# Two token tiles of the gated MLP move, for two thirds of d_ff, from plain products to steps of seven block products

## The chip, the cores and the metric

One core of a Trainium2 chip. The metric is the time of one execution on the device in microseconds; the kernel before is given as the median of three runs. The engines are TensorE (PE in the profile, its weight loads PEld), VectorE (DVE), ScalarE (ACT), GpSimd (POOL) and SyncE (SP), which issues the DMAs of this kernel.

## The reference

Attention with a memory, then a gated MLP on its output. B=4, H=8, S=576, D=64, so 2304 tokens of 512; d_ff is 1536. q, k, v, M_prev and z_prev are float32, w_a, w_b and w_out are float64, and the result is float32.

```python
def _attn_ref(q, k, v, M_prev, z_prev, beta):
    scores = scale * np.matmul(q, k.transpose(0, 1, 3, 2))
    scores = np.where(causal, -1000000000.0, scores)
    scores = scores - scores.max(-1, keepdims=True)
    a = np.exp(scores)
    a /= a.sum(-1, keepdims=True) + 1e-09
    local = np.matmul(a, v)
    q_p = phi(q)                       # phi(x) = where(x > 0, x, exp(x) - 1) + 1
    mem_ret = np.einsum('bhsd,bhde->bhse', q_p, M_prev)
    mem_norm = np.einsum('bhsd,bhd->bhs', q_p, z_prev)[..., None] + 1e-06
    g = 1.0 / (1.0 + np.exp(-beta))[None, :, None, None]
    return g * (mem_ret / mem_norm) + (1 - g) * local

def _moe_ref(x, w_a, w_b, w_out):
    return (((x @ w_a) * (x @ w_b)) @ w_out).astype(np.float32)
```

## The kernel before

**Arithmetic.** A float32 operand is split into a high part, which TensorE reads as it is, and the rest, and a product is three matmuls: high by high, high by low, low by high. ScalarE copies out the high part, VectorE subtracts it (`split_lo`, line 224).

**Order.** No scheduler runs. Every operation has a short name, and a text lists `name.index` in the order of issue, the same list for all engines; each engine takes its own in that order and waits on the others by semaphores. `HEAD`, `LOOP` and `TAIL` are that text (`schedule` unrolls `LOOP`), and after it `step7` is called in a Python loop.

**Attention (0 to 205.5 us).** Sixteen pairs of heads in a software pipeline of some 70 names a pair. The local part of each pair goes to `xs` in DRAM (`st_`). Towards its end the first unit of weights is converted.

**Weights.** The 24 units n (two for each of the twelve blocks f of 128 columns of d_ff: a with b, 128x1024, and out, 128x512) come as raw float64 by `load` and pass `mag` (ScalarE, line 883, from the raw words into the buffer `wt`, of which there is one for each kind), `clamp` (GpSimd), `shift`, `high`, `low` (VectorE, 903 and its neighbours), `hi` (ScalarE, 922) and `lo` (VectorE, 224). hi and lo write the split weights `wh`, `wl`, which stay on the chip. The next `mag` into a `wt` waits for the `lo` of the one before.

**Columns.** Tokens are cut in tiles of 384: tiles t = 0 to 3 are tokens 0 to 1535. A column (t, f) is `uA` and `uB` (`half`, line 945: twelve matmuls 128x384 each, h transposed, d_ff on partitions), `ucx` (ScalarE, a copy of b's sum to SBUF), `umx` (VectorE, times a's), `uhh`, `uhl` (the split of h) and `uo` (`outer`, line 983: nine matmuls 128x512 into three PSUM banks that hold the tile's output rows over all f; `written` carries them out). There are 48: tiles 0 and 1 by twelve f, then tiles 2 and 3 by twelve f. Until about 310 us the columns of tiles 0 and 1 run beside the conversion of the weights.

**Memory units.** Tiles 2 to 5 (tokens 768 to 2303) get their memory part from 16 units (t, j): `memory_unit`, names `q_load` to `q_join_l`. A unit loads q, z and the two halves of x, makes phi (VectorE's part at line 1131), the norm (a sum, four copies of 32x12 at line 1154, an addition, a reciprocal), transposes, splits, retrieves on TensorE, and joins (1200) the result to the sum of the two halves of x that GpSimd made (`sums`). In tiles 2 and 3 the rows are then split for the columns (`q_join_h`, `q_join_l`).

**Seven-product steps.** Tokens 1536 to 2303 (768) are multiplied by a and b in twelve calls of `step7(f)`, in Strassen and Winograd's form: the halves of x over d_model and tokens (B11 to B22) and four sums of them (T1, TT2, T4, T3; `combine`, `split_x`) against the blocks a11 to a22 (w_a and w_b, halves of d_model) and four sums s1 to s4. A product `part` is six matmuls of 384, seven in place of eight. For the sums, VectorE adds the split weights together again (`Wf`, 24 times 128x512), SP stores them (`Ws`, to `ws`), they are loaded (`sums_load`), GpSimd adds blocks (`sums_of`) and ScalarE and VectorE split them. Three sums of products begin from `p1`, the first product, which ScalarE copies to SBUF (line 1354) for VectorE to add (1371 and others). Four blocks of 128 rows of the output leave in the step (`out_rows`, 1425); the other two of each f are kept split (`kept`) and multiplied at the end (`late_rows`, 1456).

```python
        al = bank("ab")
        part(al, a11, B11, True)
        p1 = pools["w2"].tile([P, TB], F32, tag="x", name="x", bufs=1)[:, 0:TH]
        nc.scalar.activation(out=p1, in_=al, func=AF.Copy)
        ...
        be = bank("ab2")
        part(be, s2, TT2, True)
        u2 = tmp("u2")
        nc.vector.tensor_tensor(out=u2, in0=be, in1=p1, op=ALU.add)
        ...
        ga = bank("ab")
        part(ga, s1, T1, True)
        part(al, a12, B21)
        part(be, s3, T3)
```

Of the kernel before, what the change touches and what calls it, by code (L numbers as in the profile page):

```python
# [30 lines left out]
BANKS = """
0123450125341450231452304203541203541032014312345021340250432452310542305103253152401352014025124153
0421504305145341203541032014312340521430250123502301543120534513045305142013540241052405412351042532
1543254213041523403142034231052425310312401324501324015354123120543532041354014235034120512
"""
LOOP = """
Lt:-1 mag2:3 me:3 H1:2 shift1:3 b_3:1 S_3:1 py:4 m3A:1 v_l:2 low2:3 mc:1 hh:4 e4:2 h3A:3 TQ:0 thQ:0
pe:3 TK:0 H0:3 l3A:3 lo0:2 V1A:3 r_:2 V2A:3 b_:1 mx:3 tlQ:0 b_2:1 e3A:1 lo1:4 m3B:1 S_2:1 n0:2
mag1:2 ma:0 thK:0 S_:1 xA:3 V1B:3 shift2:3 n1:2 tlK:0 m2B:1 st_:4 e3B:1 Tq:0 pc:2 m2A:1 V2B:3 pb:2
n2:2 e2B:1 Lp:1 hl:4 n4:2 e2A:1 high2:3 n3:2 Lk:-2 high0:2 clamp0:2 mb:0 mB:1 eB:1 px:4 v_h:1 G2A:2  # L40
sq:-1 thq:0 G1:2 mA:1 LM:2 hi1:4 G0:2 pd:2 xB:3 h2A:2 h0:2 G2B:2 md:1 tlq:0 G5:2 high1:3 shift0:2
mu:0 h5:2 S_4:1 l2A:2 h2B:2 clamp2:3 l5:2 l2B:2 h1:2 G4:2 clamp1:3 l1:2 m4:1 eA:1 cx:3 w_0:2 pf:3
G3B:2 sm:3 hi0:2 h3B:2 h4:2 low1:3 low0:2 pa:1 Lv:0 l0:2 l3B:2 mag0:1 l4:2 G3A:2
/
clamp2 md hh v_l H1 e4 pe me mag2 Lt low2 h3A px sq mb b_3 S_3 pb Lk TQ V1A pf m3A l3A TK thQ shift2
V2A clamp1 b_ pc tlQ r_ pd b_2 e3A thK mc Lv S_2 S_ mag1 py n1 clamp0 m3B m2A V1B Lp n4 n2 Tq xA n3
m2B e3B n0 e2A H0 tlK st_ shift0 e2B thq V2B high1 mB G5 v_h mA mag0 G1 tlq eB G2B G2A xB lo1 h5 h2B
l5 h2A G4 sm S_4 l2B shift1 h1 hi0 l2A h4 G0 h0 eA w_0 l1 low1 l4 LM G3A G3B high2 pa hi1 h3B m4
high0 mx mu low0 cx hl lo0 ma l3B l0
"""  # L50
SPAN = (3, 9, 14)
TAIL = """
h3A.11 TK.14 b_3.13 l3A.11 S_3.13 pd.12 e4.12 r_.12 px.10 n3.12 pe.11 thK.14 pb.12 m3B.13 pf.11
pc.12 TQ.14 V1A.11 V2A.11 tlK.14 n1.12 m3A.13 e3B.13 thQ.14 fw.0 b_.13 b_2.13 S_2.13 n4.12 xA.11
m2A.13 Lp.13 m2B.13 e3A.13 e2A.13 S_.13 V1B.11 n0.12 e2B.13 mA.13 py.10 G5.12 V2B.11 eA.13 mB.13
tlQ.14 n2.12 G0.12 h5.12 G1.12 xB.11 l5.12 G3A.12 h1.12 v_l.12 G4.12 h3A.12 h4.12 h0.12 G2A.12
S_4.13 eB.13 pe.12 px.11 pa.13 h2A.12 v_h.13 G2B.12 w_0.12 pb.13 b_3.14 l1.12 l3A.12 h2B.12 l4.12
m4.13 py.11 S_3.14 G3B.12 l2A.12 pf.12 e4.13 TQ.15 m3A.14 r_.13 l0.12 pc.13 V1A.12 h3B.12 l2B.12
V2A.12 st_.10 thQ.15 pd.13 e3A.14 b_.14 px.12 Lv.15 l3B.12 n3.13 b_2.14 S_.14 xA.12 S_2.14 TK.15
m3B.14 n4.13 tlQ.15 Tq.14 V1B.12 n1.13 e3B.14 mA.14 V2B.12 eA.14 m2A.14 thq.14 m2B.14 e2A.14 tlq.14  # L60
G5.13 n0.13 G4.13 thK.15 mB.14 G3A.13 tlK.15 pe.13 G0.13 S_4.14 eB.14 h5.13 l5.13 n2.13 xB.12 h4.13
G1.13 h0.13 v_l.13 pf.13 Lp.14 b_3.15 pd.14 S_3.15 e2B.14 l4.13 w_0.13 m4.14 h3A.13 Tq.15 G2A.13
h1.13 l0.13 l3A.13 e4.14 thq.15 G3B.13 st_.11 l1.13 Lv.14 r_.14 h2A.13 G2B.13 m3B.15 h2B.13 V1A.13
l2A.13 e3B.15 py.12 v_h.14 n3.14 V2A.13 b_2.15 v_l.14 n4.14 b_.15 l2B.13 tlq.15 n1.14 S_2.15 m3A.15
px.13 h3B.13 l3B.13 S_.15 xA.13 e3A.15 m2B.15 pa.14 m2A.15 e2B.15 V1B.13 V2B.13 n0.14 mB.15 v_h.15
mA.15 e2A.15 pb.14 G3B.14 v_l.15 G4.14 G3A.14 eB.15 n2.14 xB.13 h3B.14 G0.14 pc.14 h4.14 l3B.14
S_4.15 G1.14 G5.14 h0.14 w_0.14 m4.15 h3A.14 eA.15 G2A.14 e4.15 h1.14 l0.14 l4.14 G2B.14 l3A.14
r_.15 to.0 pe.14 l1.14 pf.14 h5.14 h2A.14 n3.15 V1A.14 mag0.15 h2B.14 l2A.14 l5.14 n0.15 clamp0.15
n4.15 V2A.14 l2B.14 V1B.14 n2.15 n1.15 mag1.15 shift0.15 high0.15 V2B.14 xA.14 low0.15 G5.15 G2A.15
st_.12 h2A.15 G2B.15 px.14 clamp1.15 G3A.15 h5.15 G0.15 G4.15 hi0.15 h0.15 G1.15 G3B.15 l2A.15  # L70
w_0.15 h4.15 h3A.15 l5.15 lo0.15 st_.13 h1.15 l4.15 shift1.15 l1.15 H1.15 h3B.15 l3A.15 l0.15 l3B.15
xB.14 mag2.15 cx.15 V1A.15 clamp2.15 shift2.15 h2B.15 py.14 high1.15 V2A.15 l2B.15 H0.15 V1B.15
py.13 high2.15 V2B.15 low1.15 mx.15 st_.14 xA.15 xB.15 hh.15 hl.15 st_.15 low2.15 pp.0 hi1.15 lo1.15
uA.1 Khi.2 Kload.7 Kmag.3 Kload.6 uB.1 Klo.2 Kclamp.3 ucx.1 Kshift.3 Khigh.3 uA.2 Kload.8 Kmag.4
# [86 lines left out]
def kernel(  # L161
# [1465 lines left out]
```

## Time and profile before

| | us |
|---|---|
| median of three runs | 656.33 (655.96 to 656.79) |
| the profiled execution | 658.8 |
| its span in the trace | 656.9 |
| attention, up to | 205.5 |
| columns beside the conversion of the weights | 205.5 to 310 |
| columns alone, the last with the first step | 310 to about 522 |
| one seven-product step in the steady state | 10.07 |

All rows are of the profiled execution. The page's first part gives the busy time of each engine, its fourth the chain of work that ended last, its sixth the DMA issues. The windows give the same busy times for a stretch, with the granted clock of TensorE, the DMA engines' share and the GB/s moved. A group by line has the busy time and the mean of one in ns, then the idle time before and what ended it.

### The profile page before, as it was taken

The numbers are of one execution on the slowest core, as the hardware profiler recorded it, in microseconds if no ns is written. First come the engines' busy times: TensorE is split into PE (matmuls) and PEld (weight loads), VectorE is DVE, ScalarE is ACT, GpSimd is POOL, SyncE is SP. The second block draws the span as 40 slices with busy tenths as digits, with TensorE's granted clock in tenths as the row PEclk, the third lists the DMA queues.
The fourth block names the chain that finished last, engine by engine and source line by source line (L and its number), as shares of the span: only waits on it lengthen the run. The fifth ranks groups of instructions, "written<-read, shape, count | busy, mean of one in ns | idle before, by whom it ended". The sixth has DMA issues, their size and how long they took to land.

```text
span 656.9 us, 11557 instructions
## 1 busy us (share of the span) xinstructions
PE 644.9 (98%) x4010; PEld 592.4 (90%) x4010; DVE 510.8 (78%) x1018; ACT 338.0 (51%) x806; POOL 278.2 (42%) x402
## 2 busy tenths in 40 slices
PE   9999999999989999999999999999999999999998
PEld 6788889899878899999999999998999899999987
DVE  6999998988889888898997667477776676768740
ACT  6999999999976454454133223234223423123310
POOL 4999999999994122112402020011011443113200
PEclk9999999999999999999999999999999999999999
DMA  8956646466641454552445243234311321111001
GB/s 184 201 132 181 172 116 180 139 172 212 188 176 73 164 190 135 185 193 49 113 146 148 78 143 96 75 74 118 69 41 33 103 74 65 64 33 65 0 33 65
DMA packets 130250, 76.85 MB, mean 117 GB/s; under 512 B 98704, under 2 KB 117392, under 8 KB 130192
## 3 DMA queue, kind: packets, MB, share of 16 engines
q1 hardware_dynamic: 130192, 76.12, 41.0%
q8 instruction: 32, 0.52, 0.3%
q14 instruction: 26, 0.21, 0.1%
HBM read 55.64 MB, written 20.45 MB: 116 GB/s over the span
## 4 chain that ended last, share of the span: by engine, by line
PE 66%; DVE 15%; POOL 8%; ACT 6%; issue 3%; DMA 1%; SPq 1%; ACTq 0%; POOLq 0%; DVEq 0%
PE pp L945 22%; PE pp L1340 12%; PE o L983 10%; PE pt L220 5%; PE pw L734 4%; PE o L1425 4%; POOL P L634 4%; PE pt L568 3%; DVE PT L224 3%; PE pr L1456 3%; DVE wl L224 2%; DVE nm L607 2%; DVE wt L903 1%; PE m L1425 1%; POOL xf L1299 1%
## 5 line engine op out<-in xcount | busy, mean ns | idle before, releaser
L945 PE MATMUL pp<-xh,wh 128*128 128x384 f32 x376 | 127.2, 338 | 1.9 <-ACT x L958 1.1
L945 PE MATMUL pp<-xh,wl 128*128 128x384 f32 x376 | 126.1, 335 | 0.0
L945 PE MATMUL pp<-xl,wh 128*128 128x384 f32 x376 | 125.9, 335 | 0.0
L634 POOL TENSOR_SCALAR P<-P,sum 128x256 f32<-128x256 f32 (+4 forms) x144 | 82.1, 596 | 2.7 <-ACT ph L299 1.6
L1299 POOL TENSOR_TENSOR xf<-xf 128x256 f32<-128x256 f32 x48 | 39.8, 830 | 90.7 <-DMA xf<-ws 58.0
L945 PEld LDWEIGHTS pp<-xh,wh 128*128 128x128 f32 x376 | 70.6, 188 | 6.6 <-ACT x L958 3.2
L945 PEld LDWEIGHTS pp<-xl,wh 128*128 128x128 f32 x376 | 70.6, 188 | 1.3
L945 PEld LDWEIGHTS pp<-xh,wl 128*128 128x128 f32 x376 | 70.6, 188 | 0.0
L617 ACT ACTIVATE P<-pt,nm 128x128 f32<-128x128 f32 (+3 forms) x128 | 67.1, 534 | 6.7 <-DVE nm L607 3.5
L224 DVE TENSOR_TENSOR PT<-pt,PT 128x512 fp32r<-128x512 f32 (+2 forms) x112 | 62.7, 588 | 9.3 <-ACT PT L689 8.2
L734 PE MATMUL pw<-PT,vh 128*128 128x448 f32 (+4 forms) x352 | 64.1, 319 | 1.5 <-ACT xo L743 0.8
L734 PEld LDWEIGHTS pw<-PT,vh 128*128 128x128 f32 x352 | 55.9, 189 | 6.9 <-DVE PT L224 2.0
L607 DVE TENSOR_REDUCE nm<-pt 128x1 f32<-128x384 f32 (+3 forms) x128 | 55.7, 478 | 3.6 <-PE pt L568 3.1
L983 PE MATMUL o<-wh,hl 128*128 128x512 f32 x144 | 56.9, 395 | 0.0
L983 PE MATMUL o<-wl,hh 128*128 128x512 f32 x144 | 56.7, 394 | 0.0
L983 PE MATMUL o<-wh,hh 128*128 128x512 f32 x144 | 56.1, 390 | 0.0
L220 PE MATMUL pt<-ident,P 128*128 128x128 f32 (+1 forms) x400 | 52.7, 275 | 2.8 <-POOL P L634 1.4
L689 ACT ACTIVATE PT<-pt 128x512 fp32r<-128x512 f32 (+2 forms) x112 | 53.0, 529 | 3.0 <-PE pt L220 3.0
L889 POOL TENSOR_SCALAR wt<-wt 128x512 f32<-128x512 f32 (+1 forms) x21 | 21.3, 1012 | 75.5 <-ACT wt L883 75.5
L958 ACT ACTIVATE x<-pp 128x384 f32<-128x384 f32 x47 | 22.9, 487 | 56.8 <-DVE hl L224 33.9
L965 ACT ACTIVATE hh<-x 128x384 fp32r<-128x384 f32 x48 | 25.1, 522 | 49.3 <-DVE x L961 28.2
L220 PEld LDWEIGHTS pt<-ident,P 128*128 128x128 f32 (+1 forms) x400 | 43.8, 140 | 6.3 <-POOL P L634 4.3
(214 smaller groups left out, 1556.2 us busy)
## 6 DMA issues: line engine op xcount, KB each, us to landing
xs<-xo SPq DMA_DIRECT2D x16, 576.0 KB, 4.2
xx<-xs SPq DMA_DIRECT2D x32, 192.0 KB, 3.5
wr<-in_moe_w_a_dram SPq DMA_DIRECT2D x12, 512.0 KB, 4.8
wr<-in_moe_w_b_dram SPq DMA_DIRECT2D x12, 512.0 KB, 5.8
wr<-in_moe_w_out_dram SPq DMA_DIRECT2D x12, 512.0 KB, 3.9
ws<-fw SPq DMA_DIRECT2D x24, 256.0 KB, 2.3
xf<-ws SPq DMA_DIRECT2D x12, 512.0 KB, 3.2
qr<-in_q_dram SPq DMA_DIRECT2D x34, 128.0 KB, 3.4
```

Of the source, the lines that this page charges most:

```text
L220: nc.tensor.transpose(out, x, ident[0:x.shape[0], 0:x.shape[0]])
L224: eng.tensor_tensor(out=lo, in0=x, in1=hi, op=ALU.subtract)
L607: nc.vector.tensor_reduce(out=s["nm"][:, c:c + 1], in_=src, axis=AX.X, op=ALU.min)
L617: nc.scalar.activation(out=s["P", i][:, h, :], in_=src, func=AF.Exp, scale=-1.0, bias=s["nm"][:, c:c + 1], accum_out=s["sums"][:, c, 0:1],)
L634: nc.gpsimd.tensor_scalar(out=pr[:, h, :], in0=pr[:, h, :], scalar1=r[:, c:c + 1], scalar2=1.0, op0=ALU.mult, op1=ALU.mult,)
L689: nc.scalar.activation(out=dst, in_=src, func=AF.Copy)
L734: nc.tensor.matmul(pv[:, a:hi], lhsT=w, rhs=x, start=(n == 0), stop=(n == len(ops) - 1))
L945: nc.tensor.matmul(pp, lhsT=w[:, w0:w0 + P], rhs=x[:, kk, :], start=(c == 0), stop=(c == 3 * KK - 1),)
L983: nc.tensor.matmul(po[t, m], lhsT=hx[:, m * P:(m + 1) * P], rhs=w[:, w0:w0 + DM], start=(f == ORDER[t][0] and n == 0), stop=(f == ORDER[t] ...
L1299: nc.gpsimd.tensor_tensor(out=o, in0=x, in1=y, op=op)
L1340: nc.tensor.matmul(o, lhsT=a[:, kk * P:(kk + 1) * P], rhs=b[:, kk, :], start=first and c == 0, stop=True, skip_group_check=True,)
L1425: nc.tensor.matmul(po[NB, m], lhsT=hx, rhs=w, start=(f == 0 and n == 0), stop=(f == NFT - 1 and n == 2),)
```

## The change

Tokens 768 to 1535 keep columns for f 8 to 11 only: `FA = 8`, `NB = 2`. For f 0 to 7 they are multiplied in eight seven-product steps (n 0 to 7, group 0), ahead of the twelve of tokens 1536 to 2303 (n 8 to 19, group 1); the pieces of x are made twice. 48 columns become 32, twelve steps become twenty. All 16 memory units go the way that tiles 4 and 5 had, their two halves of x put together by a ScalarE copy into PSUM ahead of the retrieval (`seed`), and the four 32x12 copies move to ScalarE (`pairs`).

In a step the first product's sum is copied by ScalarE from its bank into the next (`cp1`), and the other joins are made the same way: `cu2`, `cu3`, `ch1` copy a PSUM sum to SBUF on ScalarE at the points where VectorE added `p1` before; the joins `ju3`, `jh1`, `ju2`, `jh2` stay with VectorE.

The float32 weights for the sums are stored straight from the conversion buffer (`keep`), so `Wf` and `Ws` go. The split weights of a and b are also stored (`split_keep`, four DMAs for each f), and a step reads a11, a12, a22 back (`whole_load`, two DMAs). The columns' a and b weights of f 1 to 5 lie in a pool that is closed after them. The rows of tile 2 that the columns have summed go to DRAM (`partly`) and come back as the seed of the steps' rows (`part_load`, `row_seed`) or are added at the end (`late_row`, `late_written`).

One flat text of 2881 entries, `ORDER`, takes the place of `HEAD`, `LOOP`, `TAIL` and the loop over `step7`. It also gives the attention another order, with the same operations, and has another list of PSUM banks (`BANKS`).

```diff
-HEAD = """
...
+ORDER = """
+Dk.0 zq.0 id.0 zi.0 wm.14 mk.0 mag1.1 zq.1 ib.0 b_2.0 Dq.0 TK.0 Dk.1 b_3.0 Dq.1 Eq.0 TQ.0 thK.0
...
+st_.15 pp.0 hi1.15 Khi.2 uB.1 Kload.7 hl.15 Kload.6 lo1.15 ucx.1 Kmag.3 Klo.2 uA.1 umx.1 Kclamp.3
+uo.0 Kshift.3 Khigh.3 uhh.1 Klow.3 Kmag.4 Khi.3 Kclamp.4 Kmag.5 uhl.1 Kshift.4 uB.2 Khigh.4 ucx.2
+uA.2 Klo.3 Klow.4 Kkeep.4 umx.2 uo.1 uB.3 Khi.4 uhh.2 Kclamp.5 Kmag.6 uA.3 Kshift.5 Klo.4 Kclamp.6
...
+ybe.18 hh1.17 yal.19 ru.19 hl1.17 cu2.18 ybe2.18 hl0.17 yga.18 ch1.18 or2.17 cu3.18 ybe3.18 ju3.18
...
-    NB = 4
-    START = [t * TB for t in range(NB + 2)]
+    NB = 2
+    START = [t * TB for t in range(NB + 4)]
...
+        def keep(n):
+            f = n // 2
+            nc.sync.dma_start(out=ws[f], in_=turned[n].bitcast(F32))
...
+        def split_keep(n):
+            f = n // 2
+            for i, w in enumerate(wab[f]):
+                for a, c, k in ((0, 0, 2 * Q), (2 * Q, 3 * Q, Q)):
+                    nc.sync.dma_start(out=wsa[f][:, i, a:a + k], in_=w[:, c:c + k].bitcast(F32))
...
+    FA = 8
+    START_F = {0: 0, 1: 0, NB: FA, NB + 1: FA}
...
+    def partly(m):
+        ob = ring["t"][0][:, (m - 1) * DM:m * DM] if m else None
+        written(po[NB, m], None, m % 2, ob, part_out[:, m])
...
+        def pairs():
+            half, whole, other = r["n"]
             for c in range(4):
                 c2 = c ^ 1
-                nc.vector.tensor_copy(other[Q4 * c:Q4 * c + Q4], half[Q4 * c2:Q4 * c2 + Q4])
+                nc.scalar.activation(
+                    out=other[Q4 * c:Q4 * c + Q4], in_=half[Q4 * c2:Q4 * c2 + Q4], func=AF.Copy
+                )
...
-        def sums():
-            nc.gpsimd.tensor_tensor(
-                out=r["x"][0], in0=r["x"][0], in1=r["x"][1], op=ALU.add
+        def seed():
+            pt = r["pt"] = ps_m()
+            nc.scalar.activation(
+                out=pt[:, 0:J * TW], in_=r["x"][1].rearrange("p j c -> p (j c)"), func=AF.Copy
             )
...
-    def weight_whole(n):
...
-        nc.vector.tensor_tensor(out=t, in0=wh, in1=wl, op=ALU.add)
-
-    def weight_store(n):
...
+    def whole_load(n):
+        f = group_of(n)[1]
         if f:
+            a = W6 * (2 + (n - 1) % 2)
+            for i, x in enumerate(abl):
+                nc.sync.dma_start(out=x[:, a:a + 3 * Q].bitcast(F32), in_=wsa[f][:, i])
...
+    def copied(n, o, a):
+        r = y[n]
+        if o == "be":
+            r[o] = bank("ab2")
         else:
+            tmp(n, o)
+        nc.scalar.activation(out=r[o], in_=r[a], func=AF.Copy)
+
+    def joined(n, o, a, b, op=ALU.add):
...
+        nc.vector.tensor_tensor(out=r[o], in0=r[a], in1=r[b], op=op)
...
+    def row_seed():
+        o = po["r", 0, 0] = pools["m"].tile([P, DM], F32, tag="m", name="m")
+        nc.scalar.activation(out=o, in_=held[2], func=AF.Copy)
+
+    def late_row(f, i):
         if f == 0:
...
+        three(po["late", i], kept(0, f), wout[f], i * P, f == 0, f == last_of(0))
...
-    columns += [(t, f) for t in range(2, NB) for f in ORDER[t]]
+    columns += [(t, f) for t in (NB, NB + 1) for f in range(FA, NFT)]
...
-        for f in range(NFT):
-            step7(f)
```

## Rows read from the trace of the kernel before

**Rows 1.** The page, part 1: busy us, share of the span, instructions.

```profile
PE 644.9 (98%) x4010; PEld 592.4 (90%) x4010; DVE 510.8 (78%) x1018; ACT 338.0 (51%) x806; POOL 278.2 (42%) x402
```

**Rows 2.** The page, part 4: the chain that ended last, by engine.

```profile
PE 66%; DVE 15%; POOL 8%; ACT 6%; issue 3%; DMA 1%; SPq 1%; ACTq 0%; POOLq 0%; DVEq 0%
```

**Rows 3.** Windows: stretch, length, PE, PEld, DVE, ACT, POOL busy, clock, DMA, GB/s.

```profile
22.00:104.00 82.00, 81.04 (x683) 72.29 (x682) 78.84 (x179) 78.62 (x225) 79.35 (x124) 1.00 0.67 162
104.00:185.00 81.00, 81.00 (x702) 73.87 (x701) 69.75 (x156) 76.24 (x218) 78.49 (x130) 1.00 0.63 181
185.00:205.50 20.50, 17.71 (x117) 15.81 (x116) 19.88 (x31) 13.27 (x29) 16.19 (x20) 1.00 0.32 114
205.50:310.00 104.50, 103.23 (x540) 94.88 (x539) 92.00 (x119) 52.56 (x79) 22.99 (x24) 1.00 0.44 145
310.00:430.00 120.00, 120.00 (x635) 112.54 (x634) 87.03 (x201) 34.16 (x70) 20.66 (x23) 1.00 0.40 115
552.72:562.79 10.07, 10.07 (x56) 9.54 (x55) 6.74 (x12) 2.56 (x7) 3.34 (x4) 1.00 0.15 51
```

**Rows 4.** Chain of waits: start us, us, engine, tile, line, count.

```profile
292.07 2.08 PE o L983 x9
294.15 4.18 PE pp L945 x24
...
552.72 6.24 PE pp L1340 x36
...
561.40 1.39 PE o L1425 x6
562.79 6.24 PE pp L1340 x36
```

**Rows 5.** Timeline of the conversion: start us, us, engine, line, operation.

```profile
227.31 1.22 DVE L910 SCALAR_TENSOR_TENSOR wt<-wr,wt 128x1024 uint32<-128x1024 uint32 x1
230.59 1.22 DVE L224 TENSOR_TENSOR wl<-wt,wh 128x1024 fp32r<-128x1024 f32 x1
231.84 1.12 ACT L883 ACTIVATE wt<-wr 128x1024 f32<-128x1024 f32 x1 [0.50 <-DVE wl L224]
305.31 1.23 DVE L224 TENSOR_TENSOR wl<-wt,wh 128x1024 fp32r<-128x1024 f32 x1 [0.24 <-ACT wh L922]
306.78 0.33 PE L945 MATMUL pp<-xh,wh 128*128 128x384 f32 x1
```

**Rows 6.** Waits, 205 to 305 us: waiter, releaser: us, times, longest.

```profile
ACT wt L883 <- DVE wl L224: 14.7, 15, 2.2
PEld pp L945 <- ACT x L958: 3.2, 5, 1.0
PE pp L945 <- ACT x L958: 1.1, 3, 0.6
```

**Rows 7.** The page, part 6: DMA issues, KB each, us to landing.

```profile
ws<-fw SPq DMA_DIRECT2D x24, 256.0 KB, 2.3
xs<-xo SPq DMA_DIRECT2D x16, 576.0 KB, 4.2
xf<-ws SPq DMA_DIRECT2D x12, 512.0 KB, 3.2
```

**Rows 8.** Groups by line and form, 552 to 625 and 310 to 522 us.

```profile
L1371 DVE TENSOR_TENSOR u<-u,pp 128x384 f32<-128x384 f32 x7 | 3.9, 555 | 0.2
L1354 ACT ACTIVATE x<-pp 128x384 f32<-128x384 f32 x7 | 3.4, 492 | 9.7 <-PE pp L1340 9.7
L1319 ACT ACTIVATE sh<-xf 128x768 fp32r<-128x768 f32 x4 | 3.4, 841 | 3.4 <-POOL xf L1299 3.4
L1131 DVE SCALAR_TENSOR_TENSOR ph<-q,ph 128x384 f32<-128x384 f32 x16 | 10.0, 627 | 17.0 <-ACT ph L1121 7.3 <-DMA z<-in_z_prev_dram 6.6 <-DMA xx<-xs 2.9
L1200 DVE TENSOR_TENSOR xf<-m,xf 128x384 f32<-128x384 f32 x8 | 4.3, 542 | 1.5 <-PE m L1193 1.3 <-issue 0.2
L1154 DVE COPY n<-n 32x12 f32<-32x12 f32 x64 | 11.6, 182 | 1.2
```

More of the change, by code (lines that the diff above doesn't have):

```diff
@@ L35 @@
[L35 to L41, printed above, removed]
@@ L157, in schedule @@
-    yield from named(TAIL)
+    for w in ORDER.split():
+        nm, p = w.split(".")
+        yield nm, int(p)
 @with_exitstack
@@ L1284, in sums_load @@
-    def sums_load(f):
-        if f < NFT:
-            a = 0 if f % 2 == 0 and f else 8 * Q
-            t = ring[f] = xf[0][:, a:a + 4 * Q]
-            nc.sync.dma_start(out=t, in_=ws[f])
-    def sums_of(f):
-        if f < NFT:
-            a11, a12, a21, a22 = (ring[f][:, i * Q:(i + 1) * Q] for i in range(4))
-            for o, x, y, op in (
-                (a22, a21, a22, ALU.add), (a21, a11, a21, ALU.subtract),
-                (a11, a22, a11, ALU.subtract), (a12, a12, a11, ALU.subtract),
-            ):
-                nc.gpsimd.tensor_tensor(out=o, in0=x, in1=y, op=op)
@@ new lines, in sums_h, with sums_l, bank, part @@
+    def sums_h(n):
+        nc.scalar.activation(out=sums_home(n)[0], in_=ring[n], func=AF.Copy)
+    def sums_l(n):
+        hi, lo = sums_home(n)
+        split_lo(nc.vector, lo, ring[n], hi)
+    y = {}
+    WEIGHT = {"a11": 0, "a12": 1, "a22": 2, "s2": 0, "s4": 1, "s3": 2, "s1": 3}
+    def bank(key, tag="ab"):
+        return pools[key].tile([P, DM], F32, tag=tag, name="pp")[:, 0:TH]
+    def part(n, nm, w, x, first=False):
+        r = y.setdefault(n, {})
+        if first:
+            r[nm] = bank("ab")
+        if w[0] == "a":
+            wh, wl = whole_home(n)[WEIGHT[w]]
+        else:
+            wh, wl = (z[:, WEIGHT[w] * Q:(WEIGHT[w] + 1) * Q] for z in sums_home(n))
+        xh, xl = xc[x]
+        c = 0
+        for kk in range(2):
+            for a, b in ((wh, xh), (wh, xl), (wl, xh)):
+                nc.tensor.matmul(
+                    r[nm], lhsT=a[:, kk * P:(kk + 1) * P], rhs=b[:, kk, :],
+                    start=first and c == 0, stop=True, skip_group_check=True,
+                )
+                c += 1
@@ L1442, in end, with gone @@
-        both()
-        hh()
-        hl()
-        first()
-        rest = [(pools[k].tile([P, DM], F32, tag="ab", name="pr"), a, c0, n) for k, a, c0, n in (
+        n = N7 - 1
+        joined(n, "u2", "ga", "u2")
+        joined(n, "u3", "u2", "u3", ALU.mult)
+        h_high(n, 1)
+        h_low(n, 1)
+        def gone(m):
+            row(n, m)
+            leave(po["r", 1, m], *OUT[m], START[NB + 2] + m * P, m % 2)
+        gone(0)
+        gone(1)
+        rest = [(pools[k].tile([P, DM], F32, tag="ab", name="pr"), a, c0, w) for k, a, c0, w in (
```

807 lines of the change are left out of this document (405 added, 402 removed).

## The prediction

> **What bounds the kernel now.** I read the profile in this order: busy time, the chain, the stages, the pace of the matmuls, the waits, then the rows of the operations that the change touches. TensorE is busy 644.9 of 656.9 us and every other engine 78% or less [rows 1], and the chain that ended last runs 66% through TensorE [rows 2]. The stages [rows 3] say where that holds. From 310 us on TensorE has no idle time (120.00 of 120.00). In the attention (22 to 185 us) four engines are full together: GpSimd 79.35 of 82 and 78.49 of 81, ScalarE 78.62 of 82. From 205.5 to 310 us, where the float64 weights are converted, TensorE is busy 103.23 of 104.5 but VectorE 92.00 as well. The granted clock is 1.00, the upper level, in every stretch, so no term below is about the clock.
>
> The pace is read off the chain [rows 4]: 24 matmuls of 128x384 take 4.18 us (0.174 each), nine of 128x512 take 2.08 (0.231 each). A seven-product step takes 10.07 us (552.72 to 562.79): 42 matmuls of 384, twelve of 512. It waits for nobody, so what leaves TensorE's list there leaves the time.
>
> The conversion stage has no spare time at its end: the last split of weights for a and b runs 305.31 to 306.54 [rows 5], and the product that needs it starts at 306.78. Yet TensorE waited only 1.1 and 3.2 us for ScalarE there, while ScalarE waited 14.7 us in 15 turns for the split that frees its conversion buffer [rows 6].
>
> **The change part by part.** The sum is made against the profiled execution, 658.8 us (span 656.9 and 1.9 around it); the median of the three runs, 656.33, lies 2.5 lower, and I take that off at the end.
>
> **TensorE's work.** For f 0 to 7 the two columns (tiles 2 and 3) go: 48 matmuls of 384 and 18 of 512, 2 x (4.18 + 2.08) = 12.52 us. A step comes: 42 of 384, twelve of 512 at once and six of 512 later, 10.07 + 1.39 = 11.46 us by [rows 4]. Per step 6 x 0.174 = 1.04 us are saved, over eight steps **-8.4 us**. The memory retrieval keeps its matmuls, and so do the output rows. All of this lies on the path: the chain around 300 and 560 us is matmul after matmul.
>
> **VectorE and ScalarE in a step.** VectorE loses three of seven joins (0.555 each [rows 8]), because sums start from a ScalarE copy into PSUM: 6.74 us of a step [rows 3] become 5.1. ScalarE gets three more copies of 0.492 [rows 8]: 2.56 becomes 4.0. Both fit in 10.07 us. No row shows ScalarE writing PSUM; nearest is its copy out of PSUM at 0.492, the other end the split copy of 0.841 [rows 8]; I take 0.49, the same size and source. TensorE waits for the first copy (alpha into beta's bank), and in the new order at least one product of 1.04 us stands between, so it costs nothing up to about 0.9 us. If that cover failed, 0.3 us in each of 20 steps would be 6 us.
>
> In the first eight steps eight retrieval units run beside them. A unit's ten kinds of VectorE work, 627 ns for the first and 542 for the last [rows 8], sum to 4.8 us once the four 182 ns copies have gone to ScalarE. So VectorE has 9.9 us in 11.46 of TensorE: I take 0. The turnover of the eight x pieces before step 8 is covered by sixteen kept row products of 0.69 us. GpSimd's weight sums, 3.34 us of a step [rows 3], are a third of it. The 24 additions `Wf` on VectorE and GpSimd's sums of x in the units fall away, from engines that were not last: 0.
>
> **Stored weights.** The float32 weights now leave from the conversion buffer itself, 512 KB by DMA, and the next |w| into that buffer waits for the landing. Before, it waited for the split: in one turn the low bits end at 228.53, the split ends at 231.81, and |w| starts at 231.84 [rows 5], 3.3 us after. No row shows this store. Its bounds are 2.3 us (256 KB store) and 4.2 us (576 KB store) [rows 7]; I take 4.2, the size next to it, and 0.3 for issue: 1.2 us later than now, ten times, 12 us of ScalarE waiting. Behind that waiting |w| stand ScalarE's x and hh copies, for which TensorE waits; behind the store on SP's queue stand the next weight loads and the split stores. Of the present 14.7 us of such waits 4.3 came through to TensorE, under a third, so 12 us would give 3.5; **+3**, as the new order starts the conversions a product earlier. Bounds 0 (VectorE's other work covers the hold) to +12 (all of it shifts the last split, which has no slack).
>
> The Trainium skill, DMA: Bandwidth & Descriptors (the section on where a DMA's fixed 2 us go), says that a completion comes only after the target's write receipt, and slowest from HBM, which speaks against holding a compute buffer for a store. Its fit, 2.0 us and bytes over 436 GB/s, gives an estimated 3.2 us for 512 KB; by that the hold would be 0.2 us and the term under +1. The 576 KB row, 4.2 us against 3.3 by the fit, is slower, and the sum goes by the row.
>
> The stores bring some 10 MB to a stretch that moves 145 GB/s at a share of 0.44 [rows 3]; the share would be about 0.75. I add nothing, the upper bound being in the +12.
>
> **Split weights from DRAM.** Steps read a11, a12, a22 (two loads of 384 KB) into a buffer free again two steps later. Counted in the new order, TensorE has 4.5 to 5.5 us of work between the buffer's last use and its next in five steps, 6 to 14 in the others. A 512 KB load landed in 3.2 us [rows 7]; both together I estimate at 4 to 5. **+0.5**, bounds 0 and 3.
>
> **The flat order.** It rewrites the attention too, with the same operations. Room there: the engines' 3 to 4% of 163 us, and the turn to the MLP, 185 to 205.5 us, with TensorE at 17.71 of 20.5 [rows 3]. A changed order can lose as much. Bounds -7 and +4; **-2**, under the 2.8 us that the turn leaves idle.
>
> Sum: 658.8 - 8.4 + 3 + 0.5 - 2 = 651.9, less 2.5: **649.4 us**.
>
> **The rivals.** First, **the order gives more**: the attention takes up all its slack. For it: TensorE's weight loads cover 72.29 + 73.87 of 163 us there, 90%, against 112.54 of 120, 94%, where the pace is full [rows 3]. At 94% the attention would be 7 us shorter: 656.3 - 8.4 - 7 = 641. Against it: GpSimd at 97%. 0.20. The Trainium skill, Perfetto Trace Analysis, Identifying the Most-Contended Engine, gives this reading: matmul busy time is no measure of headroom, the weight loads' share is. The trace agrees that the two differ (81.00 of 81 against 73.87).
>
> Second, **the stores hold the conversion**: from about 1.1 us per buffer turn undiminished, 11 us in the ten turns, they eat the 8.4 and the order's 2. At 1.5 us, 15 us: 656.3 - 8.4 + 15 - 1.5 = 661. For it: the last split has no slack, and VectorE has only 12.5 us idle in the stretch. Against it: two thirds of such waits now stay off TensorE. Slower 0.10, within the band 0.07.
>
> Third, **VectorE becomes the bound** in the eight steps with units: 9.9 of 11.46 us, and its waits on ScalarE's four copies; 0.5 us a step gives 653.4. Chance 0.10. It is the case where the change does not give what it says: the products go and the steps stay as long. TensorE's list has no such gap in the present steps, which speaks against it.
>
> **How the numbers follow.** The forecast has 0.53, its own range 645 to 654. Faster by over 0.2% (about what a measurement of this kernel can tell from no change), below 655.0: 0.53 + 0.20 + 0.10 = 0.83; within 0.07; slower 0.10. The range, 640.5 to 657.5, reaches to 641 and leaves out the slower rival and a tail below the first.
>
> **What would show it.** Right: 504 + 8 x 42 matmuls in steps, steps 8 to 19 at 10.1 us, the chain there all TensorE; the last split for a and b within 3 us of where it stands before the product that needs it. Wrong: ScalarE's |w| waiting on a DMA by more than 10 us and TensorE idle before 310 us; TensorE waiting for ScalarE's copy in the steps; a first MLP product more than 4 us away from 205.5, where the MLP now stands alone [rows 3].

## The result: slower by 0.5%, where faster by 1% was forecast

The changed kernel takes 660.36 us (median of five runs, 660.13 to 662.83), the kernel before 656.33 (655.81 to 657.13): a ratio of 1.0054, with an interval of 1.0032 to 1.0076. Measured a second time it was 1.0050 (1.0024 to 1.0076). The forecast was 649.4, range 640.5 to 657.5. The time lies by the second rival, 661 us, which had 0.10.

The profiled execution took 660.17 us, its span is 658.4. The page of the changed kernel, parts 1 and 6 (busy us, share, instructions; DMA issues with KB each and us to landing):

```profile
PE 639.7 (97%) x3962; PEld 585.3 (89%) x3962; DVE 490.3 (74%) x911; ACT 390.3 (59%) x941; POOL 288.2 (44%) x418
...
raw<-ws SPq DMA_DIRECT2D x20, 512.0 KB, 3.7
...
abh<-wsa SPq DMA_DIRECT2D x18, 384.0 KB, 3.5
abl<-wsa SPq DMA_DIRECT2D x18, 384.0 KB, 4.3
...
ws<-wt SPq DMA_DIRECT2D x12, 512.0 KB, 3.2
```

TensorE has 48 matmuls fewer than in [rows 1], as the change says, and yet the span is 1.5 us longer. The same stretches as in [rows 3], in the changed kernel (length; PE, PEld, DVE, ACT, POOL busy; granted clock, DMA share, GB/s):

```profile
22.00:104.00 82.00, 80.27 (x667) 70.05 (x666) 79.39 (x177) 78.00 (x222) 76.09 (x120) 1.00 0.71 160
104.00:185.00 81.00, 81.00 (x702) 74.10 (x700) 71.17 (x156) 75.20 (x216) 79.11 (x132) 1.00 0.60 161
185.00:205.50 20.50, 18.24 (x123) 15.98 (x122) 17.69 (x30) 16.24 (x36) 17.79 (x23) 1.00 0.60 209
205.50:310.00 104.50, 99.39 (x520) 91.83 (x519) 88.69 (x113) 48.19 (x73) 31.72 (x33) 1.00 0.82 268
310.00:430.00 120.00, 118.36 (x623) 110.58 (x622) 85.64 (x172) 61.80 (x146) 15.86 (x21) 0.99 0.46 128
```

Three stretches have lost. From 205.5 to 310 us, the conversion, TensorE is busy 99.39 us in place of 103.23 [rows 3], with 520 matmuls done in place of 540; the DMA share went from 0.44 to 0.82. From 310 to 430 us it is busy 118.36 us in place of 120.00, at a granted clock of 0.99. And from 22 to 104 us, in the attention, GpSimd did 76.09 us of work in place of 79.35 and TensorE 667 matmuls in place of 683, so the attention is behind.

What TensorE and ScalarE waited for between 207 and 320 us (us in all, times, longest):

```profile
PE pp L1027 <- ACT x L1040: 3.6, 1, 3.6
PE pp L1027 <- DVE x L1043: 1.1, 1, 1.1
...
ACT wt L959 <- DMA ws<-wt: 12.1, 4, 5.1
...
ACT wt L959 <- DVE wl L300: 7.6, 5, 3.3
```

The first line of [rows 6] is split here: part of the turns still wait for the low split, and four of them, 12.1 us, for the landing of the store. How the longest of them reaches TensorE, from the timeline of the changed kernel (start us, us, engine, line, operation; in brackets the idle time before and what ended it):

```profile
296.59 3.45 SPq L1165 DMA_DIRECT2D z<-in_z_prev_dram  x4
297.98 1.23 DVE L986 SCALAR_TENSOR_TENSOR wt<-wr,wt 128x1024 uint32<-128x1024 uint32 x1
300.74 0.38 SPq L999 DMA_DIRECT2D ws<-wt  x1
306.41 1.12 ACT L959 ACTIVATE wt<-wr 128x1024 f32<-128x1024 f32 x1 [5.14 <-DMA ws<-wt]
307.42 0.48 ACT L1040 ACTIVATE x<-pp 128x384 f32<-128x384 f32 x1
307.96 0.44 PE L1027 MATMUL pp<-xh,abh 128*128 128x384 f32 x1 [3.59 <-ACT x L1040]
309.82 0.52 PE L1027 MATMUL pp<-xh,abl 128*128 128x384 f32 x1
```

The float32 weights are complete at 299.21 (297.98 + 1.23). The store is issued at 300.74, since SP was issuing loads of z and of weights until then, and lands 5.2 us later. Only then does ScalarE take the next |w|, which starts 5.7 us after the issue; behind it in ScalarE's queue stands the copy of a PSUM sum, and for that bank TensorE waits (3.6 us in the row; 3.75 counted from the start of the matmul before at the full pace). The last line shows what the stop cost beyond itself: the matmul of 128x384 takes 0.52 us. From 309.0 to 312.5 us TensorE's granted clock was 0.51, the lower of its two levels, and matmuls started every 0.32 us in place of 0.174.

A table helps with the runs below. It splits each trace at the first product of the MLP in the banks `pp` and at the start of TensorE's last matmul, both read off TensorE's rows (us; the rest, to the end of the span, is 3.4 before and 3.5 in all the others):

| trace | first product | MLP |
|---|---|---|
| before | 205.4 | 448.2 |
| changed | 207.6 | 447.2 |
| before, second trace | 205.2 | 447.1 |
| changed, second trace | 208.6 | 447.6 |
| \|w\| of unit 22 later | 210.5 | 445.4 |
| stores that read x | 209.1 | 441.8 |
| old attention, first placing | 214.0 | 446.2 |
| no trips of split weights | 208.5 | 440.2 |
| two buffers | 208.1 | 442.9 |
| two buffers, old attention | 205.5 | 441.6 |
| the same, no trips | 205.5 | 439.6 |
| the same, five names moved | 210.7 | 440.7 |
| before, with the stores | 206.3 | 483.2 |

### The profile page after: what moved, and what is told of

Its sections match the earlier page's. It is cut to its first block, busy times and chain, and to the rows that moved or that the text cites. A ratio compares the mean times of both kernels' runs of the same rounds, so it can differ in the third digit from the quotient of the medians.

```text
span 658.4 us, 11639 instructions
## 1 busy us (share of the span) xinstructions
PE 639.7 (97%) x3962; PEld 585.3 (89%) x3962; DVE 490.3 (74%) x911; ACT 390.3 (59%) x941; POOL 288.2 (44%) x418
## 5 line engine op out<-in xcount | busy, mean ns | idle before, releaser
L1354 POOL TENSOR_TENSOR raw<-raw 128x256 f32<-128x256 f32 x80 | 67.0, 840 | 186.9 <-DMA raw<-ws 138.3
L710 POOL TENSOR_SCALAR P<-P,sum 128x384 f32<-128x384 f32 (+4 forms) x144 | 82.6, 594 | 6.3 <-DVE sum L702 5.0
L683 DVE TENSOR_REDUCE nm<-pt 128x1 f32<-128x128 f32 (+3 forms) x128 | 56.2, 478 | 4.7 <-PE pt L644 3.6
L1027 PE MATMUL pp<-xh,abh 128*128 128x384 f32 x160 | 54.6, 341 | 4.7 <-ACT x L1040 3.6
L1027 PE MATMUL pp<-xh,abl 128*128 128x384 f32 x160 | 54.4, 340 | 0.0
L1027 PE MATMUL pp<-xl,abh 128*128 128x384 f32 x160 | 54.2, 339 | 0.0
L1402 DVE TENSOR_TENSOR u<-pp,u 128x384 f32<-128x384 f32 x40 | 22.1, 553 | 40.1 <-PE pp L1381 34.2
L1396 ACT ACTIVATE u<-pp 128x384 f32<-128x384 f32 x40 | 19.6, 489 | 39.0 <-PE pp L1381 28.1
L959 ACT ACTIVATE wt<-wr 128x1024 f32<-128x1024 f32 (+1 forms) x24 | 21.8, 909 | 28.2 <-DMA ws<-wt 12.1
L1381 PE MATMUL pp<-xh,abh 128*128 128x384 f32 x112 | 37.6, 336 | 0.4 <-ACT pp L1396 0.4
L1064 PE MATMUL o<-wl,hh 128*128 128x512 f32 x96 | 37.9, 395 | 0.0
L1381 PE MATMUL pp<-xh,abl 128*128 128x384 f32 x112 | 37.7, 337 | 0.0
L1381 PE MATMUL pp<-xl,abh 128*128 128x384 f32 x112 | 37.6, 336 | 0.0
```

Source lines behind the costliest of these rows:

```text
L683: nc.vector.tensor_reduce(out=s["nm"][:, c:c + 1], in_=src, axis=AX.X, op=ALU.min)
L710: nc.gpsimd.tensor_scalar(out=pr[:, h, :], in0=pr[:, h, :], scalar1=r[:, c:c + 1], scalar2=1.0, op0=ALU.mult, op1=ALU.mult,)
L1027: nc.tensor.matmul(pp, lhsT=w[:, w0:w0 + P], rhs=x[:, kk, :], start=(c == 0), stop=(c == 3 * KK - 1),)
L1064: nc.tensor.matmul(po[t, m], lhsT=hx[:, m * P:(m + 1) * P], rhs=w, start=(f == START_F[t] and n == 0), stop=(f == NFT - 1 and n == 2 and t ...
L1354: nc.gpsimd.tensor_tensor(out=o, in0=x, in1=y, op=op)
L1381: nc.tensor.matmul(r[nm], lhsT=a[:, kk * P:(kk + 1) * P], rhs=b[:, kk, :], start=first and c == 0, stop=True, skip_group_check=True,)
```

## The experiments

The theory after the result (A): the buffer held by the store makes ScalarE wait, and what stands behind it in its queue stops TensorE. Rivals: the traffic itself (B), and the new order of the attention (C). Every ratio is against runs of the kernel before on the same chip; three groups of runs were made, with medians of before of 656.99, 658.16 and 658.40 us.

### One name later

```diff
-... Klo.20 uhh.14 Kkeep.20 Kmag.21 uA.15 Kclamp.21 uhl.14 Kmag.22 Kshift.21 ucx.15 ...
+... Klo.20 uhh.14 Kkeep.20 Kmag.21 uA.15 Kclamp.21 uhl.14 Kshift.21 ucx.15 Kmag.22 ...
```

> One name of the changed kernel's order moves: the |w| of weight unit 22 (ScalarE, it waits 5.1 us for the landing of a 512 KB store) stands behind ScalarE's copy of column 15's sum instead of ahead of it. Theory A, the store's wait costs only where a PSUM copy is queued behind it: TensorE's 3.75 us stop at 304 us goes, and with it the 1.5 us in which its matmuls ran at the lower clock; 660.4 - 5 = 655.4 us. Rival B, the held buffer delays the whole conversion, so the next wait comes up later by as much: 659.5 to 660.5 us.

660.6 us, ratio 1.0064 (1.0042 to 1.0085): no gain that can be measured. TensorE's waits from 205.5 to 320 us in this run:

```profile
PE o L1054 <- DVE hl L290: 2.7, 3, 2.0
PE pp L1017 <- DVE x L1033: 1.4, 1, 1.4
```

The stop of 3.6 us behind the copy is gone, and no lower clock is seen. In its place stand waits of 2.0 and 1.4 us for VectorE, which gets its words later. Rival B of this run (the next wait comes up later) has most of it: ScalarE still waited 10.7 us for stores. Cutting one link was not enough. In this trace the MLP is 1.8 us shorter than in the changed kernel's first one and the first product 2.9 us later, so a small gain in the conversion is not excluded.

### The hold taken away

```diff
         def keep(n):
             f = n // 2
-            nc.sync.dma_start(out=ws[f], in_=turned[n].bitcast(F32))
+            src = turned[n] if n < 4 else xhl[0][0].rearrange("p k c -> p (k c)")[:, 0:2 * DM]
+            nc.sync.dma_start(out=ws[f], in_=src.bitcast(F32))
```

> The stores of the float32 weights for f 2 to 11 keep size, place and queue but read the rows of x, which nobody overwrites in that stretch, so that no |w| waits for a landing; the output is not the reference's. Theory A, the hold is what costs in the conversion: the stops at 276 us (1.3), 304 us (3.75) and the lower clock after it (1.5) go, 653.5 to 655 us, and no stretch below 2.4 GHz. Rival B, it is the traffic (268 GB/s at a DMA share of 0.82 there), which is unchanged: 659 to 660.5 us.

654.34 us, ratio 0.9962 (0.9941 to 0.9982), within what theory A expected. All transfers were still there (DMA share 0.80, 264 GB/s), and TensorE had next to no idle time in the conversion. The window of this run:

```profile
205.50:310.00 104.50, 104.13 (x548) 96.50 (x548) 93.31 (x119) 50.94 (x77) 32.41 (x33) 1.00 0.80 264
```

### The old attention, first try

The list of names up to the first of the MLP (`pp`) and the list of banks are those of before; the two stores that the change adds in this part stand behind `low0` and `low2`.

```diff
+... high0.15 V2B.14 xA.14 low0.15 keep0.15 G5.15 G2A.15 st_.12 h2A.15 ... lo0.15 st_.13 ...
```

> The changed kernel with the attention part of the order and its list of PSUM banks as in the kernel before; the two new stores of that part stand behind the low bits of their units. Theory C, the new order of the attention costs time by itself: the first product of the MLP stands at 205.4 to 206 us instead of 207.6 and the time falls by 2 us, to 658.4. Rival, the two added stores and the earlier weights are what lengthen the attention: 207 to 208 us and 660.4 us.

667.47 us, ratio 1.0165 (1.0149 to 1.0182). Neither expectation: the first product came at 214.0 us. Waits of ScalarE and SP from 186 to 214 us, and SP's timeline:

```profile
ACT xo L814 <- DMA xs<-xo: 9.3, 1, 9.3
...
SPq L994 <- DVE wt L960: 10.4, 1, 10.4
```

```profile
194.82 0.34 SPq L994 DMA_DIRECT2D ws<-wt  x1
195.26 13.52 SPq L821 DMA_DIRECT2D xs<-xo  x3
```

SP stood 10.4 us before the new store, waiting for the low bits, and the attention's output store of pair 12 behind it, which had long been ready (185.3 us in the kernel before). Its buffer was not free, ScalarE waited 9.3 us for it and TensorE 9.8 for ScalarE. This says nothing of the order of the attention; it shows that a store costs by what is queued behind it on SP, too.

### Without the trips of the split weights

```diff
         def split_keep(n):
+            return
...
-        if f:
+        if f < 0:
             a = W6 * (2 + (n - 1) % 2)
             for i, x in enumerate(abl):
                 nc.sync.dma_start(out=x[:, a:a + 3 * Q].bitcast(F32), in_=wsa[f][:, i])
```

> The stores of split weights and their loads in the steps are left out (some 20 MB of transfers; the steps multiply whatever lies in the buffers). Theory B, traffic slows the loads and stores that somebody waits for: the 512 KB stores land in 3 us instead of up to 5.5, the stop at 304 us shrinks by 2 us or more and the time is 656 to 658. Theory A, the order of ScalarE's queue: a shorter landing helps by what it shortens at 304 us, under 1.5 us: 659 to 660.

654.06 us, ratio 0.9961 (0.9946 to 0.9975): more than either expected. Here the single buffer is still held, but ScalarE waits less for it:

```profile
ACT wt L959 <- DMA ws<-wt: 7.3, 3, 3.5
```

The turn that cost most in the changed kernel, here (timeline):

```profile
298.99 0.35 SPq L999 DMA_DIRECT2D ws<-wt  x1
303.48 1.13 ACT L959 ACTIVATE wt<-wr 128x1024 f32<-128x1024 f32 x1 [2.43 <-DMA ws<-wt]
```

That is 7.3 us where the changed kernel has 12.1 (14.1 in its second trace). The landings are much alike: the median of the twelve stores is 3.3 us here and 3.2 with the trips, the longest 4.8 and 5.2. What changed is the turn that cost most. Here SP issues the store as soon as its weights are complete (298.97 us) and the next |w| starts 4.5 us later; with the trips SP came to it 1.5 us late and the |w| started 5.7 us after the issue. So hold and trips are not two causes that add up: the trips make SP late and this landing longer, and the hold turns both into waiting. What each costs alone needed a kernel without the hold that keeps its results.

### Two more traces as they are

> The kernel before once more, for a second trace of it: its first one took 658.8 us where the median of its runs is 656.3. If the 2.5 us are stops that come and go (0.8 us at 209 us, 0.8 at 445, 1.1 at 522), this trace shows a span of 654 to 655 us without them; if a trace always costs 2 us more, it shows 657 again.

> The changed kernel as it is, on the chip of the other runs of this group: 660 to 661 us, with the stop at 304 us and the lower clock after it.

The kernel before: a span of 655.7 us, the run 657.52. The stops at 209 us (0.8), 443 (1.6) and 521 (1.3) came again; those between 222 and 303 us, 1.4 us in all in the first trace, did not. So about half of the 2.5 us can be stops that come and go, and the first trace was one of the slower executions; the median of before is itself 658.16 us in this group. The changed kernel: 661.75 us, ratio 1.0050 (1.0024 to 1.0076), with a stop of 3.3 us at 306 us; the clock stayed at 1.00 this time. That is the rarer case: in 13 of the 15 executions of the changed kernel the mean granted clock over the span was 0.994 to 0.997.

### A second conversion buffer

```diff
+            if n in (6, 10, 14, 18):
+                t = turned[n] = pools["w"].tile([P, w], U32, tag="w10", name="wt2")
+            elif n == 22:
+                t = turned[n] = ring["t"][1].bitcast(U32)
+            else:
-            t = turned[n] = pools["w4"].tile([P, w], U32, tag="wt" + c, name="wt", bufs=1)
+                t = turned[n] = pools["w4"].tile([P, w], U32, tag="wt" + c, name="wt", bufs=1)
...
+            if n == 21 and f not in wout:
+                two = pools["w"].tile([P, 2 * DM], F32R, tag="w10", name="w10")
+                wout[f] = [two[:, 0:DM], two[:, DM:2 * DM]]
...
```

> The changed kernel with a second conversion buffer: units 6, 10, 14 and 18 turn their words in the place that unit 21's split takes later, unit 22 in a buffer of the steps, so that |w| waits for the store of two units before; the output is the reference's and all transfers stay. If the hold of the buffer is what costs (theory A): like the run whose stores read x, 654 to 655 us, and faster than before by 0.3%. If that run gained because its stores no longer had to wait for the low bits on SP's queue: 658 to 660.

655.9 us, ratio 0.9963 (0.9941 to 0.9985): as with the stores that read x, and faster than before. From 1.0050 to 0.9963 are 0.87%, 5.7 us; the MLP alone went from 447.6 to 442.9 us in the traces, 4.7. This is the price of the hold, with every transfer in place: the 658 to 660 us of the rival, SP's queue, did not come. The second buffer also spares |w| the wait for the low split of the unit before, 5.3 us of ScalarE's time in the changed kernel; the stores that read x left 3.5 us of that and gained as much. In all ten executions the mean granted clock was 0.999 to 1.000, so the price includes the fall of the clock.

### The old attention, second try

```diff
+... lo0.15 st_.13 keep0.15 h1.15 l4.15 ...
```

> The second buffer, and the attention's order of before, with the first store of float32 weights behind the output store of pair 13 on SP's queue (ahead of the one of pair 12 it made ScalarE wait 9.3 us for a buffer of the output). If the new order of the attention costs by itself (theory C): first product of the MLP at 205.5 to 206.5 us and 1.5 to 3 us less than with the second buffer alone. If the two stores of this part cost wherever they stand: no gain, first product at 207.5 or later.

652.39 us, ratio 0.992 (0.9885 to 0.9954), the first product at 205.5 us in place of 208.1. The stretch from 22 to 104 us with two buffers, then with two buffers and the old attention:

```profile
22.00:104.00 82.00, 80.00 (x664) 69.92 (x664) 79.50 (x178) 77.82 (x221) 75.94 (x119) 1.00 0.72 160
```

```profile
22.00:104.00 82.00, 81.05 (x686) 72.44 (x685) 78.82 (x179) 78.71 (x226) 79.29 (x124) 1.00 0.67 164
```

With the old order GpSimd is as full as in [rows 3] (79.29 us, 79.35 there), with the new one it has 3.3 us less done by 104 us. How long GpSimd waited for VectorE's sums from 22 to 185 us (us, times, longest), with two buffers, then with the old attention too:

```profile
POOL P L710 <- DVE sum L702: 4.9, 7, 1.4
```

```profile
POOL P L705 <- DVE sum L697: 1.1, 4, 0.3
```

In the six traces with the new order GpSimd's busy time from 22 to 104 us is 75.94 to 76.19 us, in the traces with the old one 78.98 to 79.39, save one, of 74.75, in which the clock fell as well. Theory C is borne out, for the order and the list of banks together: 0.43%, 2.8 us, and 2.6 in the traces. Which names cost it stays open. The intervals of the two ratios overlap, so the size leans on the traces; and that one trace with the old order is the last but one row of the table (first product at 210.7 us).

### One thing of the change alone, in the kernel before

```diff
+        def keep(n):
+            nc.sync.dma_start(out=wheld[n // 2], in_=turned[n].bitcast(F32))
...
-... Klo.21 Klow.22 Kload.23 Kmag.23 ...
+... Klo.21 Klow.22 Kkeep.22 Kload.23 Kmag.23 ...
```

> The kernel before, and one thing of the change alone: behind the low bits of each unit of a and b from unit 4 on, its conversion buffer is stored to DRAM (ten stores of 512 KB that nobody reads), so that the next |w| into it waits for a landing. Theory A, the held buffer is what lost the gain: ScalarE waits some 12 us for these landings and the time rises by 4 to 7 us, to 660.5 to 663.5. Rival, it takes the changed order or the traffic of the split weights beside it: 656 to 658.

694.15 us, ratio 1.0545 (1.051 to 1.058): not 4 to 7 us but 36. Its windows, then ScalarE's and TensorE's waits from 205 to 345 us:

```profile
205.50:310.00 104.50, 86.58 (x428) 79.66 (x427) 71.45 (x95) 41.50 (x62) 17.73 (x18) 0.93 0.44 150
310.00:345.00 35.00, 26.67 (x118) 24.05 (x117) 20.62 (x28) 10.73 (x17) 6.54 (x9) 0.85 0.53 155
```

```profile
ACT wt L880 <- DMA wheld<-wt: 31.2, 7, 7.9
...
ACT wt L880 <- DMA wr<-in_moe_w_b_dram: 6.8, 1, 6.8
ACT wt L880 <- DMA wr<-in_moe_w_out_dram: 6.2, 1, 6.2
...
PE pp L945 <- ACT x L958: 25.5, 8, 7.7
```

Ten stores that nobody reads, at a median landing of 3.3 us (the longest 7.7), made ScalarE wait 31.2 us. Of TensorE's 25.5 us five stops, 17.3 us, stand behind these waits. Two more, 7.6 us, stand behind ScalarE's waits of 6.8 and 6.2 us for loads of raw weights, which had stood behind a store on SP's queue, and the eighth, 0.6 us, is in the kernel before as well. The granted clock went down to 0.93 and 0.85 over whole stretches. So one kind of store holds two things up, its buffer and SP's queue, and this run does not part them. That the changed kernel's own order of the conversion had taken most of the price off, down to the 6 us above, is a reading: no run shows that order alone.

### What is left of the trips, and of the order in the steps

> The version with two buffers and the attention's order of before, without the stores of split weights and their loads in the steps (the steps multiply what lies in the buffers). With the single buffer that took 6 us away. If the trips cost mainly by making the held store land later, they cost little once nothing is held: 0.5 to 1.5 us less than that version. If they cost by themselves, on SP's queue and in the steps: 3 us less or more.

The edit is the one shown above, in the version with two buffers and the old attention. 651.14 us, ratio 0.9888 (0.9855 to 0.992), 0.32% or 2.1 us less than with the trips, between the two expectations; the MLP is 2.0 us shorter in the trace. Without the hold the trips cost 2 us, with it 6. The intervals overlap here as well. Read the other way, the same runs say that the hold costs 5.7 us beside the trips and about 2 without them (0.9961 against 0.9888, less the 0.43% of the attention; 0.6 us by the MLP of the two traces), which is not told apart from nothing. So of the 7.8 us that hold and trips cost together some 4 arise only where both are there.

```diff
-... uB.29 rl.0 Ksplit_keep.22 ru.0 ucx.28 co.6 uA.29 umx.28 uhh.28 ru.1 yal.0 ... cp1.0 q_phi2.9 ucx.30 uA.30 sl.6 q_x_load.8 rs.0 ...
+... uB.29 ru.1 rl.0 Ksplit_keep.22 ru.0 ucx.28 co.6 uA.29 umx.28 uhh.28 yal.0 ... cp1.0 rs.0 q_phi2.9 ucx.30 uA.30 sl.6 q_x_load.8 ...
...
-... umx.27 q_phi.8 uo.26 q_join.7 uhh.27 ... q_pairs.9 q_seed.8 ... q_phi.12 yga2.2 ... cp1.3 ...
+... umx.27 uo.26 q_join.7 uhh.27 q_phi.8 ... q_seed.8 q_pairs.9 ... yga2.2 ... cp1.3 q_phi.12 ...
```

> The version with two buffers and the attention's order of before, and five names moved: GpSimd's weight sums of step 1 ahead of those of step 0, the low part of step 0's sums ahead of a memory unit's and a piece's work on VectorE, two first steps of memory units (which wait for a load of q) behind the copies that TensorE waits for, one copy into PSUM ahead of four small ones. If the stops at 381, 402, 411 and 474 us in that version's trace are only the queues' order: 1.5 to 2.5 us less. If they are the engines' load: the stops come back elsewhere and under 0.7 us is left.

653.06 us, ratio 0.9895 (0.9859 to 0.993). Against 0.992 this is not told apart; in the trace the MLP is 0.9 us shorter. The stops at 381, 402 and 411 us are gone, and TensorE's longest wait from 205 to 560 us is another one, in the conversion:

```profile
PE o L1067 <- DVE hl L295: 1.5, 1, 1.5
```

Both this version and the one without the five moves beat the kernel before and the changed one, by 0.8 to 1.0% and by 1.3 to 1.5%.

## Why the prediction was wrong, point by point

**TensorE's work, right.** 48 matmuls are gone, and the last step begins 10.09 us after the one before it, where the kernel before had 10.07. The MLP of the version without hold and trips, 439.6 us, is the 447.1 to 448.2 of before less 8.4, within 1 us: no cost of the steps themselves is left over. That TensorE has no idle time from 310 us on holds for the row that was read, 310 to 430 us; later in that trace stand two stops of 0.7 and 0.8 us.

**VectorE and ScalarE in a step, right as to size.** ScalarE's copy into PSUM, which no row of before showed, takes 472 ns where 0.49 us was taken. Groups of the changed kernel from 430 to 560 us, the copy into PSUM and one of the same shape to SBUF:

```profile
L1396 ACT ACTIVATE u<-pp 128x384 f32<-128x384 f32 x22 | 10.8, 491 | 16.0 <-PE pp L1381 12.1 <-DVE u L1402 2.0 <-DVE hl L300 1.9
...
L1396 ACT ACTIVATE pp<-pp 128x384 f32<-128x384 f32 x11 | 5.2, 472 | 13.6 <-PE pp L1381 9.2 <-DVE h L1402 3.2 <-DVE xf L1265 1.0
```

TensorE waited for it 0.4 us in all from 395 to 500 us, and 1.3 once for a split of sums on VectorE. The third rival, VectorE as the bound, did not come: from 430 to 460 us, beside the memory units, TensorE is busy 30.00 of 30 us and VectorE 22.63.

**Three terms failed.** Of the 10.2 us between the forecast of -6.9 and the +3.3 that were measured, the flat order has 4.8, the stored weights 2.7 and the split weights 1.6; the rest, 1.1, stays open. The shares of the last two go by the order in which the runs took them away: the other way round the hold has cost about 2 us and the trips 5.8.

**Stored weights, mis-sized.** The mechanism was named: the next |w| waits for the landing, and ScalarE's copies stand behind it. The term was +3 and measured 5.7. That ScalarE waited 12.1 us for the stores (14.1 in the second trace) where 12 us of added waiting were forecast is luck: ten equal turns of 1.2 us were taken, from a landing of 4.2, and there were four, of 1.6 to 5.1 us, at a median landing of only 3.2. The longest is by a store that SP issued 1.5 us late behind loads and that landed after 5.2 us, in a stretch with a DMA share of 0.82. The Trainium skill, DMA: Bandwidth & Descriptors, Anatomy of one DMA, gave an estimated 3.2 us by its fit, which the page makes for DMAs issued by GpSimd. The median here, of DMAs issued by SP, is the same, and the fit says nothing of the turn that cost most.

Two steps from there did not hold. The prediction had no term for the clock ("no term below is about the clock"): the stop of 3.6 us behind the longest turn is already more than the whole term, and the lower clock after it added 1.5 us. And the discount, "under a third" of such waits coming through, was misread. Its 4.3 us add the matmuls' 1.1 to the weight loads' 3.2 [rows 6], which tell of the same stops, and they go with waits of at most 2.2 us. Longer waits came through otherwise. In the changed kernel's first trace and in the kernel before with the stores, the waits for stores of up to 3.2 us left TensorE stops of at most 1.2 us each, and those of 4.7 to 7.9 us stops of 1.5 to 7.7 us. In all 4.7 of 12.1 us came through in the one and 17.3 of 31.2 in the other. A ratio taken from short waits was used on long ones.

**Split weights from DRAM, undersized.** +0.5 with an upper bound of 3 for TensorE's waits in the steps; measured 2.1 without the hold. But TensorE hardly waited for these loads: with two buffers and the old attention its waits over 0.2 us from 320 us on name ScalarE and VectorE, the longest 1.1, 0.5 and 0.5 us, and none of these three is there without the trips, nor, with them, once the five names had moved. What the term did not have is what the trips do to SP's queue and the stores while a buffer is held: 6 us in that case. The traffic was put at nothing beside the hold, and the two terms were added as if each stood alone; together they were taken as 3.5 and measured 7.8.

**The flat order, wrong sign.** -2 was taken, with bounds of -7 and +4; it cost 2.8, the largest of the misses. The term was taken from idle time, 3 to 4% of the engines' and 2.8 us at the turn, and nothing was worked out of what the new order does with it. GpSimd was at 97% there [rows 3], and with the new order it waited 4.9 us for VectorE's sums in place of 1.1. The same row spoke against the first rival and should have spoken against the -2.

**The sum.** -8.4 + 5.7 + 2.8 + 2.1 = +2.2 us. Measured were 0.50 and 0.54%, 3.3 and 3.5 us. The missing 1.1 to 1.3 us are within the intervals, which are 1.4 to 1.7 us to either side; the order of the names in the steps (0.9 us in a trace) may be part of them and could not be told apart.

**The second rival** had the time, 661 us, in part by luck: it has 15 us of the hold and an order that helps by 1.5, where the runs show 5.7, an order that costs 2.8 and 2.1 of the trips. Its mechanism is among the causes, and its chance of 0.10 was too small. Two of the signs that were named against the forecast, ScalarE's |w| waiting more than 10 us on a DMA and TensorE idle before 310 us, both came.

## What to carry to other kernels

A store whose source is a compute buffer adds its landing to that buffer's turn. In the traces here the price is not the mean landing but the longest, with everything that is queued in order behind the waiting instruction, and behind the store on SP: look for the PSUM copy behind it, and give the buffer a twin before moving names about. Do not carry a share of covered waits from short waits to long ones; here those over 4.6 us came through by a third to nearly the whole of their length. Two terms that use the same queue are not summed as if each stood alone. A new order for a stage that was full before is a risk with its own term, and is best tried alone.

## What the runs showed of the hardware

A stop of TensorE can cost more than its length. After the stop of 3.6 us at 304 us the granted clock fell at about 309.0, and ten matmuls ran at the lower level, 1.5 us longer in all; the kernel before with the stores lost the clock five times, with mean clocks of 0.93 and 0.85 over its two stretches. After a stop of nearly the same length at the same place in the changed kernel's second trace, 3.2 us in the row, it did not fall. The Trainium skill, TensorE: Matmul & The Clock Gate, in the part on HAM oscillation, says that a wait for a DMA between tiles takes the clock down, so that the next tile starts at the lower one. The traces agree in part: in two of the five falls of the kernel before with the stores the clock was at 0.50 some two us before the matmuls started again (at 258.6 and 339.7 us), but in the changed kernel's first trace the matmuls started again at 308.0 us, a microsecond before the fall, and in its second trace none ran slow.

The end of the attention varies between executions of one order, from 205.5 to 210.7 us in three traces with the same old one. The late one, with the five names moved, is 5.2 us later. In it an operation of VectorE on 128x8 took 2.08 us at 31 us and 2.50 at 91 us, where the trace with two buffers and the old attention has 0.28 and 0.54. Beside each TensorE stopped for 1.8 us, and after the second stop the clock was at 0.50 from 96 to 99 us. The second operation, and the stop's end:

```profile
91.39 2.50 DVE L387 SCALAR_TENSOR_TENSOR rn<-rn,over_gate 128x8 f32<-128x8 f32 x1
...
94.49 0.27 PE L291 MATMUL pt<-ident,P 128*64 128x128 f32 x1 [1.82 <-POOL PT L772]
```

Why the operation took so long was not looked into.
